# A gelu's square left in its PSUM bank: ScalarE writes it over the product, and VectorE reads it there

## Chip, cores and metric

The kernel runs on one core of one Trainium2 chip. The metric is the device time of one execution in microseconds (us); lower is better. A core has five engines that work side by side: TensorE (PE), which multiplies matrices and writes its products to PSUM; VectorE (DVE); ScalarE (ACT); GpSimd (POOL); and SyncE (SP), whose queue issues here all the transfers (DMAs) between the memory outside the core and SBUF, the core's working memory.

## The reference

```python
def _A_ref(x, wqkv, wo):                      # sliding-window attention: 32 heads of 16, window 256
    qkv = ...(x @ wqkv)...
    scores = einsum("bhqd,bhkd->bhqk", q, k) * Dh ** -0.5
    p = softmax(where(0 <= i - j < 256, scores, -1e9))
    return (p @ v) @ wo

def _B_ref(x, w1, b1, w2, b2):                # dense layer with gelu (tanh form)
    h = gelu(x @ w1 + b1)
    return h @ w2 + b2

g = sigmoid((x * gate_w).sum(-1))
return g * _A_ref(...) + (1 - g) * _B_ref(...)
```

x is 2048 x 512, w1 512 x 1792, w2 1792 x 512, all in float32.

## The kernel before

Dense products are made of three matmuls in a fast 32-bit format (`mm3`, L109 to L111: high times high, high times low, low times high), so each operand is kept as a high and a low part.

The program is one order of instructions written out by hand. Each function, at the point where it is called, emits instructions to the engines' queues; `after(ns, fn)` puts a later step into a list that is ordered by a planned time, and `tick` moves the planned time on. So the place of each instruction on its engine is fixed when the program is built, and on the chip each engine works through its queue in that order, waiting on semaphores.

The work falls into these parts. First come the products with `wqkv` and the transposes of x. From about 150 us on, attention and the dense layer are interleaved. Attention has, for each block of keys, a score matmul whose maximum VectorE takes (tile `sm`, L522; its maximum `jm`, `M`, L527), a second score matmul whose exponential ScalarE takes (tile `st`, L567; exponential `pt`, L589), masks of that exponential on GpSimd (L583), and the products with v (`pv_sm`, `pv_st`, L611). On PE the steps of attention stand between groups of three matmuls of the dense layer. Last comes the product with `wo` and the output.

The dense layer is done in eight turns (`mlp`): a half of the 14 tiles of hidden units, for one of four stretches of 512 rows. A turn has a u stage and a y stage. In the u stage, PE makes seven tiles `u` (128 hidden units x 512 rows, 12 matmuls each), and each goes through `gelu`. In the y stage, PE makes four tiles `y` from the seven results `h`. The tiles u and y take turns in two PSUM banks (pool tag `d`, 2 buffers): the first matmul of a tile has to wait until the tile two places before it has been read for the last time.

`gelu` has seven steps, the first planned at once and the others 700 to 7000 ns after it, by `GELU`:

- L722, ScalarE: x1 = u + b1, from PSUM to SBUF
- L725, ScalarE (f1): the square of (u + b1), from PSUM to the SBUF tile `sq`
- L728, VectorE (f2): sq = (sq + c) * x1
- L731, ScalarE: tanh of it
- L734, VectorE: x1 = (tanh + 1) * x1
- L737, ScalarE, and L740, VectorE: the high and the low part of the result, `h`

The profile calls the tile x1 `x1h` and the tile sq `sqh`. The two buffers of `sq` also hold results of the y stage (`yo`, L815) until they are stored. L183 on VectorE or GpSimd makes the low part of a weight that has landed (`raw_w`), after ScalarE (L179) has made the high part; L665 on VectorE scales an attention result with the reciprocal `rb`, which comes by a DMA.

Of the kernel before, what the change touches and what calls it, by code (L numbers as in the profile page):

```python
# [12 lines left out]
AF = mybir.ActivationFunctionType  # L13
ALU = mybir.AluOpType
# [13 lines left out]
GC = 1.0 / 0.044715  # L28
# [4 lines left out]
def gated_mix(ctx: ExitStack, tc: tile.TileContext, x, wqkv, wo, w1, b1, w2, b2, gate_w, out):  # L33
    nc = tc.nc
# [11 lines left out]
    def f32(ap):  # L46
        return ap.bitcast(F32)
# [26 lines left out]
    b1c = cs.tile([128, NF], F32, name="b1c")  # L74
# [41 lines left out]
    def after(ns, fn, *args):  # L116
        now[1] += 1
        heapq.heappush(todo, (now[0] + ns, now[1], fn, args))
# [599 lines left out]
    def gelu(p, f, h):  # L718

        x1 = sb.tile([128, T], F32, tag="x1", bufs=2, name=f"x1{h.name}")  # L720
        sq = sb.tile([128, T], F32, tag="sq", bufs=2, name=f"sq{h.name}")
        nc.scalar.activation(x1, p, AF.Identity, bias=b1c[:, f:f + 1])  # L722

        def f1():
            nc.scalar.activation(sq, p, AF.Square, bias=b1c[:, f:f + 1])  # L725

        def f2():
            nc.vector.scalar_tensor_tensor(sq, sq, GC, x1, op0=ALU.add, op1=ALU.mult)  # L728

        def f3():  # L730
            nc.scalar.activation(sq, sq, AF.Tanh, scale=GS)  # L731

        def f4():
            nc.vector.scalar_tensor_tensor(x1, sq, 1.0, x1, op0=ALU.add, op1=ALU.mult)  # L734

        def f5():
            nc.scalar.activation(h[:, 0], x1, AF.Copy)  # L737

        def f6():
            nc.vector.tensor_sub(h[:, 1], x1, f32(h[:, 0]))  # L740
            done.add(h.name)
        for ns, fn in zip(GELU, (f1, f2, f3, f4, f5, f6)):
            after(ns, fn)
# [303 lines left out]
```

## Time and profile before

| | |
|---|---|
| median of 3 runs | 749.54 us (749.44 to 749.55) |
| span of the profiled execution, first to last instruction | 747.5 us |
| busy: PE, VectorE, ScalarE, GpSimd | 732.3, 519.5, 421.8, 372.5 us |
| granted clock of TensorE | 1.00 in all stages shown |
| DMA | 172 MB, mean 230 GB/s |

The profiled execution has no run time of its own beside the span of 747.5 us; the 2.0 us up to the median of the runs lie around the first and the last instruction.

How to read it: "busy" is the time in which an engine worked on an instruction. Matmuls are pipelined, so PE can count as busy while the next matmul is held up for a moment. The chain of work that ended last is followed back from the last instruction, at each step to what released it. In a row of a group, `out<-in` are tiles by the program's names, then come their sizes, the count, the busy time in us and the mean time of one in ns, and the idle time of the engine just before them with what ended it. In a row of the timeline, the first number is the start and the second the length, in us; a bracket at the end gives the idle time of the engine before it and what ended that.

### The profile page before, as it was taken

The numbers are of one execution on the slowest core, as the hardware profiler recorded it, in microseconds if no ns is written. First come the engines' busy times: TensorE is split into PE (matmuls) and PEld (weight loads), VectorE is DVE, ScalarE is ACT, GpSimd is POOL, SyncE is SP. The second block draws the span as 40 slices with busy tenths as digits, with TensorE's granted clock in tenths as the row PEclk, the third lists the DMA queues.
The fourth block names the chain that finished last, engine by engine and source line by source line (L and its number), as shares of the span: only waits on it lengthen the run. The fifth ranks groups of instructions, "written<-read, shape, count | busy, mean of one in ns | idle before, by whom it ended". The sixth has DMA issues, their size and how long they took to land.

```text
span 747.5 us, 17960 instructions
## 1 busy us (share of the span) xinstructions
PE 732.3 (98%) x6129; PEld 604.7 (81%) x6129; DVE 519.5 (69%) x1567; ACT 421.8 (56%) x972; POOL 372.5 (50%) x846
## 2 busy tenths in 40 slices
PE   8999999998999999999999999999999999999998
PEld 7888888876788888888887877888888888867786
DVE  4632425799768867886898689768867986784552
ACT  4434532358437835764695478437745853794550
POOL 4200000339756865876587668747765875630000
PEclk9999999999999999999999999999999999999999
DMA  9979898898995687799566889996799789558673
GB/s 318 336 243 408 288 391 282 254 311 194 263 258 132 173 238 205 178 220 265 155 169 156 237 209 232 257 231 154 179 262 238 185 204 287 138 179 230 205 235 113
DMA packets 179259, 172.12 MB, mean 230 GB/s; under 512 B 56672, under 2 KB 122976, under 8 KB 179168
## 3 DMA queue, kind: packets, MB, share of 16 engines
q1 hardware_dynamic: 179168, 170.97, 82.0%
q8 instruction: 49, 0.80, 0.5%
q14 instruction: 42, 0.34, 0.2%
HBM read 108.53 MB, written 62.39 MB: 229 GB/s over the span
## 4 chain that ended last, share of the span: by engine, by line
PE 85%; DVE 4%; DMA 3%; ACT 3%; issue 3%; POOL 1%; SPq 0%; DVEq 0%; ACTq 0%; POOLq 0%
PE sm L522 9%; PE st L567 8%; PE pv_sm L611 7%; PE y L109 7%; PE y L110 6%; PE y L111 6%; PE u L109 5%; PE u L110 5%; PE u L111 5%; PE qk L109 4%; PE qk L111 4%; PE qk L110 4%; PE a L109 2%; PE v L109 2%; PE v L111 2%
## 5 line engine op out<-in xcount | busy, mean ns | idle before, releaser
L527 DVE CUSTOM_DVE_ANT_0 jm<-sm,mask 128x320 bf16<-128x320 f32 (+4 forms) x512 | 237.9, 465 | 95.4 <-PE sm L522 61.0
L583 POOL TENSOR_SCALAR_AFFINE_SELECT pt<-pt 64x256 f32<-64x256 f32 (+1 forms) x538 | 227.6, 443 | 109.4 <-ACT pt L589 99.1
L589 ACT ACTIVATE pt<-st 128x320 f32<-128x320 f32 (+4 forms) x512 | 199.6, 424 | 139.0 <-PE st L567 135.4
L522 PE MATMUL sm<-kd,qd 96*128 96x320 f32 (+4 forms) x512 | 153.9, 312 | 6.9 <-DVE M L527 6.1
L567 PE MATMUL st<-qs,ks 128*128 128x320 f32 (+4 forms) x512 | 154.0, 309 | 1.9 <-ACT pt L589 1.9
L549 POOL CAST qs<-tt 4x256 fp32r<-4x256 f32 x256 | 124.2, 485 | 53.2 <-DVE tt L542 42.6
L522 PEld LDWEIGHTS sm<-kd,qd 96*128 96x128 f32 x512 | 96.4, 188 | 33.6 <-DVE M L527 14.2
L567 PEld LDWEIGHTS st<-qs,ks 128*128 128x128 f32 x512 | 97.1, 190 | 18.9 <-ACT pt L589 3.3
L109 PE MATMUL y<-w,h 128*128 128x512 f32 x224 | 88.6, 395 | 0.0
L110 PE MATMUL y<-w,h 128*128 128x512 f32 x224 | 87.9, 392 | 0.0
L111 PE MATMUL y<-w,h 128*128 128x512 f32 x224 | 87.9, 392 | 0.0
L109 PE MATMUL u<-mx,w 128*128 128x512 f32 x196 | 80.0, 408 | 0.0
L110 PE MATMUL u<-mx,w 128*128 128x512 f32 x196 | 77.3, 395 | 0.0
L111 PE MATMUL u<-mx,w 128*128 128x512 f32 x196 | 77.0, 393 | 0.0
L611 PE MATMUL pv_sm<-pt,vbuf 64*32 64x320 f32 (+4 forms) x1408 | 73.6, 346 | 0.2
L611 PE MATMUL pv_st<-pt,vbuf 64*32 64x320 f32 (+4 forms) x1408 | 73.3, 346 | 0.0
L611 PEld LDWEIGHTS pv_sm<-pt,vbuf 64*32 64x32 f32 x1408 | 50.2, 106 | 20.1 <-issue 2.4
L326 DVE TENSOR_TENSOR qke<-qk,qke 128x512 fp32r<-128x512 f32 x32 | 22.0, 688 | 45.9 <-ACT qke L323 38.5
L323 ACT ACTIVATE qke<-qk 128x512 fp32r<-128x512 f32 x32 | 19.1, 597 | 55.4 <-PE qk L111 32.9
L111 PEld LDWEIGHTS y<-w,h 128*128 128x128 f32 x224 | 42.1, 188 | 9.9
L339 POOL MEMSET vx<- 128x32 f32 x16 | 2.4, 156 | 89.4 <-DMA SQ<-qke 42.4
L611 PEld LDWEIGHTS pv_st<-pt,vbuf 64*32 64x32 f32 x1408 | 46.1, 106 | 0.0
(148 smaller groups left out, 1332.6 us busy)
## 6 DMA issues: line engine op xcount, KB each, us to landing
kd<-SK SPq DMA_DIRECT2D x32, 384.0 KB
qs<-SQ SPq DMA_DIRECT2D x64, 192.0 KB
mx<-XT SPq DMA_DIRECT2D x24, 512.0 KB
SQ<-qke SPq DMA_DIRECT2D x16, 512.0 KB
SK<-qke SPq DMA_DIRECT2D x16, 512.0 KB
ND<-nd SPq DMA_DIRECT2D x32, 256.0 KB
raw_w<-in_B_w_dram SPq DMA_DIRECT2D x28, 256.0 KB
ks<-SK SPq DMA_DIRECT2D x32, 192.0 KB
```

The costliest lines, as they stand in the source:

```text
L109: nc.tensor.matmul(p, lh, rh, start=first, stop=False)
L110: nc.tensor.matmul(p, lh, rl, start=False, stop=False)
L111: nc.tensor.matmul(p, ll, rh, start=False, stop=last)
L323: nc.scalar.activation(e[:, h], p, AF.Copy)
L326: nc.vector.tensor_sub(e[:, 1 - h], p, f32(e[:, h]))
L522: nc.tensor.matmul(p[:, :w], qd[0:96, n, pr, 128 * j:128 * (j + 1)], kd[0:96, n, pr, k1 - w:k1], start=True, stop=True)
L527: nc.vector.tensor_tensor_reduce(junk[:, :w], p[:, :w], mask[:, 320 - w:320], 1.0, -3e38, ALU.add, ALU.max, M[:, 2 * (b % RB) + hb, pr:pr ...
L549: nc.gpsimd.tensor_copy(dst, src.unsqueeze(1).broadcast_to([4, 2, RB, 32]))
L567: nc.tensor.matmul(p[:, :w], ks[:, slot(g_, kb // NB), pr, at:at + 128], qs[:, pr, k0:k0 + w], start=True, stop=True)
L583: nc.gpsimd.affine_select(out=v, in_=v, pattern=[[0, v.shape[1]], [1 - 2 * e, 64]], compare_op=ALU.is_ge, fill=0.0, base=-e, channel_multi ...
L589: nc.scalar.activation(pt[:, hf, pr, :w], p[:, :w], AF.Exp, scale=SCALE)
L611: nc.tensor.matmul(pv[r // 64][32 * i:32 * i + 32, q - c * T:e - c * T], vts[g_, b // NB][r:r + 64, v:v + 32], rhs(r), start=start, stop=s ...
```

## The change

Two lines of `gelu`: ScalarE writes the square over its own input, in the PSUM bank p of the tile u, and VectorE's step f2 reads it there. The tile sq in SBUF is first written by f2.

```diff
         def f1():
-            nc.scalar.activation(sq, p, AF.Square, bias=b1c[:, f:f + 1])
+            nc.scalar.activation(p, p, AF.Square, bias=b1c[:, f:f + 1])

         def f2():
-            nc.vector.scalar_tensor_tensor(sq, sq, GC, x1, op0=ALU.add, op1=ALU.mult)
+            nc.vector.scalar_tensor_tensor(sq, p, GC, x1, op0=ALU.add, op1=ALU.mult)
```

Every engine has the same instructions in the same order as before; operands and waits differ. On PE, in the u stage of the fifth turn (at 441.6 us of the profile before), this is the first matmul of the fourth tile of the turn, u_10, which takes the bank of u_8:

```order
 L522 MATMUL sm_13_2_6384<-kd,qd 128x320 [waits DVE_49]
 L567 MATMUL st_1_3_6389<-qs,ks 128x320 [waits Activation_49]
-L109 MATMUL u_10_6393<-mx_4403,w_10_5446 128x512
+L109 MATMUL u_10_6393<-mx_4403,w_10_5446 128x512 [waits DVE_49]
 L110 MATMUL u_10_6393<-mx_4403,w_10_5446 128x512
 L111 MATMUL u_10_6393<-mx_4403,w_10_5446 128x512
```

It has not moved; it now waits for VectorE, which has to be done with f2 of u_8. Before, it had no mark for ScalarE's f1, which an earlier wait of PE covered. In all, 21 first matmuls of a tile are marked with a wait for VectorE in this way.

On VectorE at the same place, f2 of u_8 stands between the product of an attention result with its reciprocal (L665, which waits for DMAs) and the low part of a weight (L183):

```order
 L527 ISA M_12_6213 128x1
 L665 TENSOR_TENSOR num_1_6194<-num_1_6194,rb_1_6196 128x512 [waits DMAHW7_49,DMAHW0_49]
-L728 SCALAR_TENSOR_TENSOR sqh_8_6322_6329<-sqh_8_6322_6329,x1h_8_6322_6328 128x512 [waits Activation_49]
+L728 SCALAR_TENSOR_TENSOR sqh_8_6322_6329<-u_8_6182,x1h_8_6322_6328 128x512 [waits Activation_49]
 L183 TENSOR_TENSOR w_9_6354<-raw_w_6177,w_9_6354 128x512 [waits DMAHW4_49,Activation_49]
 L527 ISA jm_13_0_6361,M_12_6213<-sm_13_0_6359,mask 128x320 [waits DVE_49,PE_49]
```

Only f2's first input has changed, from the SBUF tile to the bank.

On ScalarE, f1 of the same tile (the second of its turn) had a wait for the store of an earlier result from the buffer of sq; it now has none:

```order
 L722 ACTIVATE x1h_8_6322_6328<-u_8_6182,b1c 128x512
-L725 ACTIVATE sqh_8_6322_6329<-u_8_6182,b1c 128x512 [waits DMAHW3_49]
+L725 ACTIVATE u_8_6182<-u_8_6182,b1c 128x512
 L179 ACTIVATE w_9_6354<-raw_w_6177 128x512 [waits DMAHW4_49]
 L589 ACTIVATE pt_1_6345<-st_1_0_6346 128x320 [waits PE_49,Pool_49]
```

The queues of GpSimd and SyncE are the same to the last wait.

## The prediction

> **What bounds the kernel now.** I read the page first: busy time, then the chain of work that ended last, then the groups. After that came the stages, and last the moments at which TensorE (PE) stood still. A quoted row begins with its start in us from the span's start, then its length in us.
>
> ```profile
> span 747.5 us, 17960 instructions
> ...
> PE   732.3 (98%) x6129; PEld 604.7 (81%) x6129; DVE 519.5 (69%) x1567; ACT 421.8 (56%) x972; POOL 372.5 (50%) x846
> ...
> PE 85%; DVE 4%; DMA 3%; ACT 3%; issue 3%; POOL 1%; SPq 0%; DVEq 0%; ACTq 0%; POOLq 0%
> ```
>
> PE carries 85% of the chain, and an instruction that is not on PE counts only where PE waits for it. VectorE (DVE) is busy 69% on average. The stages differ (columns: stretch, its length, then busy us of PE, weight loads, DVE, ScalarE (ACT), GpSimd (POOL)):
>
> ```profile
> 254.00:288.00 34.00, 34.00 (x343) 28.43 (x341) 23.54 (x83) 16.05 (x39) 22.93 (x60) 1.00 0.87 243
> ...
> 426.00:459.00 33.00, 31.49 (x303) 25.30 (x303) 28.46 (x89) 24.81 (x57) 20.70 (x43) 1.00 0.85 214
> ```
>
> The first is a stage of second matmuls (y) with hardly any gelu: PE never stops. The second is a stage of first matmuls (u) with gelu: DVE is 86% busy and PE idle 1.5 us. What the change can move lies in the u stages.
>
> **The change, part by part.** I call the square f1 (L725, ACT) and the step that reads it f2 (L728, DVE). No instruction is added, removed or moved: PE, DVE, ACT, POOL and SP (with every DMA) issue the same list. Three things differ.
>
> *f2 reads one operand from PSUM.* Its group (busy us and mean ns), and min/median/max ns of it and of a relative:
>
> ```profile
> L728 DVE SCALAR_TENSOR_TENSOR sqh<-sqh,x1h 128x512 f32<-128x512 f32 x56 | 42.5, 759 | 2.8 <-ACT sqh L725 2.2
> ```
>
> ```profile
> L728 DVE SCALAR_TENSOR_TENSOR sqh<-sqh,x1h x56: 651/692/1578, 156.0 to 671.8; 128x512 f32<-128x512 f32 x56
> ```
>
> ```profile
> L815 DVE SCALAR_TENSOR_TENSOR yo<-y,ya x32: 651/685/692, 197.5 to 697.7; 128x512 f32<-128x512 f32 x32
> ```
>
> L815 is f2's operation with its first input in PSUM and its second in SBUF, which is what f2 becomes. Its minimum and median are f2's, but it is never above 692 ns, while f2, with both inputs in SBUF, reaches 1578. I take 685: 56 x (759 - 685) = 4.1 us of DVE time, of which only what PE waits for counts. Bounds for one f2: 651 from below, and from above 752, from the output's step, which reads PSUM too but takes a column as its scalar:
>
> ```profile
> L882 DVE SCALAR_TENSOR_TENSOR ao<-a,g,ao x17: 483/750/752, 703.3 to 744.4; 128x512 f32<-128x512 f32 x15, 128x256 f32<-128x256 f32 x2
> ```
>
> Which slowed f2 stands in an unbroken run of DVE work that PE then waits for? Five. The largest:
>
> ```profile
> 159.75 1.58 DVE L728 SCALAR_TENSOR_TENSOR sqh<-sqh,x1h 128x512 f32<-128x512 f32 x1
> ```
>
> ```profile
> 159.28 1.51 POOL L183 TENSOR_TENSOR w<-raw_w,w 128x512 fp32r<-128x512 f32 x1 [6.88 <-ACT w L179]
> ```
>
> ```profile
> 161.80 0.42 PE L522 MATMUL sm<-kd,qd 96*128 96x320 f32 x1 [0.67 <-DVE M L527]
> ```
>
> ```profile
> 172.40 0.63 ACT L179 ACTIVATE w<-raw_w 128x512 fp32r<-128x512 f32 x1 [0.49 <-DMA raw_w<-in_B_w_dram]
> ```
>
> f2 runs beside a POOL instruction of 1.5 us, and PE's score matmul (sm) waits behind it: 1.58 - 0.685 = 0.9 us. But at 172.40 ACT waits for a weight to land, which may take the lead back; I count half, 0.45, and keep 0 and 0.9 as ends. The others:
>
> ```profile
> 441.41 0.88 DVE L728 SCALAR_TENSOR_TENSOR sqh<-sqh,x1h 128x512 f32<-128x512 f32 x1
> ...
> 442.06 0.40 PE L111 MATMUL u<-mx,w 128*128 128x512 f32 x1
> ...
> 443.22 0.07 DVE L527 DVE_READ_ACCUMULATOR2_ANT M<- 128x1 f32 x1
> ...
> 443.35 0.41 PE L522 MATMUL sm<-kd,qd 96*128 96x320 f32 x1 [0.89 <-DVE M L527]
> ```
>
> ```profile
> 466.46 0.85 DVE L728 SCALAR_TENSOR_TENSOR sqh<-sqh,x1h 128x512 f32<-128x512 f32 x1
> ```
>
> ```profile
> 467.78 0.41 PE L522 MATMUL sm<-kd,qd 96*128 96x320 f32 x1 [0.62 <-DVE M L527]
> ```
>
> ```profile
> 394.97 0.77 DVE L728 SCALAR_TENSOR_TENSOR sqh<-sqh,x1h 128x512 f32<-128x512 f32 x1
> ```
>
> ```profile
> 398.93 0.41 PE L522 MATMUL sm<-kd,qd 96*128 96x320 f32 x1 [0.91 <-DVE M L527]
> ```
>
> ```profile
> 594.83 0.88 DVE sqh L728
> ...
> 604.32 0.72 POOL pt L583
> ```
>
> Against 0.685 they give 0.20, 0.17, 0.08 and 0.20. The last stands in the chain, which goes from it over ACT to POOL's masks, for which the next p.v matmuls wait. Sum of f2: 0.45 + 0.65 = 1.10 us. Where these waits go, PE's own stream is late next.
>
> *f1 writes PSUM.* No ACT instruction here writes PSUM. The nearest rows are a read that changes side:
>
> ```profile
> L323 ACT ACTIVATE qke<-qk 128x512 fp32r<-128x512 f32 x32 | 19.1, 597 | 55.4 <-PE qk L111 32.9 <-issue 10.8 <-DMA SQ<-qke 2.6
> ...
> L731 ACT ACTIVATE sqh<-sqh 128x512 f32<-128x512 f32 x56 | 35.3, 631 | 1.8 <-DVE sqh L728 1.7
> L725 ACT ACTIVATE sqh<-u,b1c 128x512 f32<-128x512 f32 x56 | 38.8, 693 | 0.0
> ...
> L233 ACT ACTIVATE ks<-nil,own 128x512 fp32r<-128x512 f32 x8 | 5.3, 724 | 0.0
> ```
>
> Reading PSUM in place of SBUF is 34 ns shorter; I take as much for the write. Ends: 597 (the fastest full-width activation, -96) and 724 (the slowest, +31). On the chain f1 stands 8 times in a piece of over 0.3 us; first and last:
>
> ```profile
> 186.53 0.59 ACT sqh L725
> ...
> 670.12 0.58 ACT sqh L725
> ```
>
> 8 x 34 = 0.27 us gained, with ends of +0.25 (longer) and -0.77. The waits that f1 loses, for the store of an earlier result from its old buffer, f2 had already; no idle time of ACT stood before f1 (0.0 above), so they cost nothing and give nothing.
>
> *The bank comes free later.* Two PSUM banks serve u and y in turn, so the first matmul of the tile after next waited for f1, and now for f2. Queued behind it on PE are the sm and st matmuls of attention, and behind those the maxima on DVE and the exponentials on ACT. I set the end of all 56 f2 against the first matmul that takes over their bank. In 53 f2 ends sooner, the tightest of these by 0.28 us:
>
> ```profile
> 662.02 0.88 DVE L728 SCALAR_TENSOR_TENSOR sqh<-sqh,x1h 128x512 f32<-128x512 f32 x1
> ```
>
> ```profile
> 663.18 0.40 PE L109 MATMUL u<-mx,w 128*128 128x512 f32 x1
> ```
>
> The three late ones, beside the f2 of 441.41 above:
>
> ```profile
> 441.60 0.39 PE L109 MATMUL u<-mx,w 128*128 128x512 f32 x1
> ```
>
> ```profile
> 666.72 0.42 DVE L577 TENSOR_TENSOR pt<-pt,cut 128x256 f32<-128x256 f32 x1
> 667.05 0.68 DVE L728 SCALAR_TENSOR_TENSOR sqh<-sqh,x1h 128x512 f32<-128x512 f32 x1
> ```
>
> ```profile
> 667.01 0.39 PE L109 MATMUL y<-w,h 128*128 128x512 f32 x1
> ...
> 671.08 0.41 PE L567 MATMUL st<-qs,ks 128*128 128x320 f32 x1 [1.20 <-ACT pt L589]
> ```
>
> ```profile
> 166.26 0.68 DVE L728 SCALAR_TENSOR_TENSOR sqh<-sqh,x1h 128x512 f32<-128x512 f32 x1
> ...
> 166.76 0.39 PE L109 MATMUL u<-xt,w 128*128 128x512 f32 x1
> ```
>
> ```profile
> 170.88 0.39 PE L567 MATMUL st<-qs,ks 128*128 128x320 f32 x1 [0.40 <-ACT pt L589]
> ```
>
> f2 ends at 442.29, 667.73 and 166.94: PE is late by 0.69, 0.72 and 0.18 us, plus 0.06 each to hear of it (443.29 to 443.35, above): 1.77 in all. Each cover is a wait of PE soon after it. At 443.35 the sm waits for DVE work queued behind this same f2; at 671.08 an st waits 1.20 for ACT; at 170.88 one waits 0.40. All are longer than the lateness, so I take 0; with the covers gone it is 1.77. The reason is general: an f2 is late when DVE is behind, and then its maxima are late too, for which PE waits anyway.
>
> A rule that speaks against the change is in the Trainium skill, "Perfetto Trace Analysis", section "Optimizing Scalar/DVE Operations": an access costs VectorE about 60 ns in SBUF and about 125 in PSUM, and ScalarE about 93 and 51. By it f2 would be 65 ns longer than an unslowed one and f1 42 shorter. An estimate from these figures, at the places above (f2 at 0.75 there), is 0.79 + 8 x 0.042 = 1.13 us less, 748.4. The L815 row disagrees for VectorE (685 against 692 in the median); the 34 ns are near its ScalarE difference.
>
> **The sum.** 1.10 + 0.27 - 0 = 1.37 us less. The profiled execution spans 747.5 us; the runs' median is 749.54, and I take the 2.0 us around the span as unchanged. 749.54 - 1.37 = 748.2.
>
> **The rivals.**
>
> (a) *More than the counted places gain.* DVE leads the u stages at 86%, and a DVE lead carries from one wait to the next. If half of the 4.1 us and the whole 0.27 reach the end, it is 749.54 - 2.3 = 747.2. Against it: even in the u stage shown, DVE is idle 14% of the time, and a lead ends at the next idle time. 17 in 100.
>
> (b) *Hidden anyway.* The lead at 161.80 is lost at 172.40, later ones to DMA landings like the one DVE waits for ahead of the f2 of 441.41: 749.54 - 0.3 = 749.2.
>
> ```profile
> 440.76 0.72 DVE L665 TENSOR_TENSOR num<-num,rb 128x512 f32<-128x512 f32 x1 [1.35 <-DMA rb<-RD]
> ```
>
> 11 in 100.
>
> (c) *PE waits for f2: slower.* The same row shows the danger: f2 can stand behind a DMA, and PE then waits for the bank. If none of the three is covered, and only 0.3 of the gains remains, 749.54 + 1.77 - 0.3 = 751.0. It decides from the point where the next wait of PE is shorter than f2's lateness. 17 in 100.
>
> (d) *PSUM reads are slow on DVE.* With f2 at 0.75, the five places give 0.41 (half of 0.83), 0.13, 0.10, 0.02 and 0.13, with f1's 0.27 together 1.06 us: 748.5. The L815 row speaks against it; 3 in 100.
>
> My forecast has 52 in 100, half of it on each side of 748.04, since the start's 0.9 comes whole or not at all. About 0.2% (1.5 us) is what a measurement of this kernel tells from no change. Faster: 26 + 17 = 43; within: 26 + 11 + 3 = 40; slower: 17. Range: 746.6, below (a), to 751.0, at (c).
>
> **What would show it.** f2's maximum at or below 700 ns and its mean near 685; f1 at 655 to 665; the idle time before the sm at 161.80 gone; rows of PE u or y L109 that wait for DVE sqh L728, under 1 us in all, and behind each a wait of PE that is shorter than before. The prediction is wrong if those waits sum to over 2 us, if f1 is over 724 ns, or if DVE falls by 4 us and PE's idle time does not move.

## The result, and the profile after

The change makes the kernel faster: 744.98 us in the median of six runs (743.49 to 745.76), against 749.54 for the kernel before (748.57 to 751.22). The ratio is 0.993, with a 95% interval of 0.9915 to 0.9945. The forecast was 748.2, and the range ended at 746.6: the sign was right, but the gain is 4.6 us and not 1.4. The profiled run of the changed kernel took 745.76, the slowest of its six, so the two traces show only 3.5 us of the 4.6 (spans of 747.5 and 744.0). In the runs of the changed kernel the time is 1.7 to 1.8 us longer than the span, so the profiled execution of the kernel before, with no run time of its own, stands for one of about 749.3 us.

The page of the changed kernel, with span, busy time and the shares of the chain:

```profile
span 744.0 us, 17964 instructions
...
PE 731.7 (98%) x6129; PEld 604.6 (81%) x6129; DVE 513.6 (69%) x1567; ACT 421.0 (57%) x972; POOL 356.9 (48%) x846
...
PE 86%; DVE 4%; DMA 4%; ACT 3%; issue 2%; SPq 1%; DVEq 0%; ACTq 0%
```

PE works as long as before. DVE is 5.9 us less busy, and POOL, none of whose instructions was touched, is 15.6 us less busy (372.5 before). That second number is the surprise. The same two stretches as before, a y stage and a u stage:

```profile
254.00:288.00 34.00, 34.00 (x342) 28.45 (x341) 23.86 (x86) 15.02 (x38) 22.97 (x61) 1.00 0.88 239
...
426.00:459.00 33.00, 32.00 (x303) 25.23 (x302) 28.86 (x90) 25.63 (x57) 22.65 (x46) 1.00 0.85 206
```

PE's idle time in the u stage went from 1.5 to 1.0 us (the same stretch of time; the changed kernel is some 3 us further in its work there). The two edited instructions, f2 and then f1 (least, median and greatest ns):

```profile
L728 DVE SCALAR_TENSOR_TENSOR sqh<-u,x1h x56: 652/685/694, 156.1 to 667.2; 128x512 f32<-128x512 f32 x56
```

```profile
L725 ACT ACTIVATE u<-u,b1c x56: 642/662/744, 154.6 to 665.5; 128x512 f32<-128x512 f32 x56
```

No f2 is held up any more: the greatest fell from 1578 to 694. What PE waited for (us in total, times, longest), first before, then after:

```profile
PE sm L522 <- DVE M L527: 6.1, 11, 1.0
PE st L567 <- ACT pt L589: 1.9, 3, 1.2
```

```profile
PE sm L522 <- DVE M L527: 3.0, 7, 0.8
...
PE st L567 <- ACT pt L589: 1.0, 3, 0.5
PE y L109 <- DVE sqh L728: 0.6, 1, 0.6
...
PE u L109 <- DVE sqh L728: 0.4, 1, 0.4
```

The waits for maxima and exponentials fell by 4.0 us, and the new waits for the bank are 1.0. GpSimd's masks as a group, before and after (busy us and mean ns of one):

```profile
L583 POOL TENSOR_SCALAR_AFFINE_SELECT pt<-pt 64x256 f32<-64x256 f32 (+1 forms) x538 | 227.6, 443 | 109.4 <-ACT pt L589 99.1
```

```profile
L583 POOL TENSOR_SCALAR_AFFINE_SELECT pt<-pt 64x256 f32<-64x256 f32 (+1 forms) x538 | 215.3, 420 | 119.0 <-ACT pt L589 108.6
```

The same 538 masks take 12.3 us less. I sorted them, by the start and end of each, into those that overlap an f2 by more than 50 ns and the rest. Before, 47 lay beside one, with a mean of 613 ns, and the rest had 426. After, 57 lie beside one, with a mean of 389, and the rest have 424.

The rest is not undisturbed: many of these masks run beside another DVE step that reads two tensors from SBUF (L734, L740, L183, L665, L577). Take the 334 masks of 64x256 alone. Before, 215 of them overlap neither an f2 nor one of these steps, and each takes 406 to 419 ns; the other 119 take 640 in the mean. After, with f2 no longer one of the steps with two tensors in SBUF, 252 are clear of such steps, again 406 to 419 ns each, and 82 are not, with 638. The 30 that meet the new f2 and no such step take 410.5 in the mean, as if f2 were not there. So a mask beside a step with two tensors in SBUF is as slow as before; there are fewer of them.

**Where the time came from.** I set the start of every first matmul (L109) after against the same one before. PE's lead in us, at times of the kernel before:

| at | lead | what added to it |
|---|---|---|
| 162 | 0.9 | f2 of 159.75 no longer held up |
| 176 | 1.8 | the subtraction L740 of 172.88 no longer held up |
| 189 | 2.1 | small steps |
| 234 | 2.4 | p.v matmuls that waited for masks |
| 395 | 3.4 | 0.4 at 322 and 0.4 at 394.5, where an sm had waited for a maximum, and small steps |
| 441.6, then 444.4 | 3.0, then 3.7 | from 3.5: a wait for the bank, given back at once, and 0.2 more as the f2 of 441.41 is not held up |
| 468 | 3.7 | 0.2 gained at 458, 0.4 lost at 465 to 467, 0.15 gained behind the f2 of 466.46 |
| 607 | 4.4 | p.v matmuls that waited for masks |
| 667.0, then 671.3 | 3.8, then 4.5 | a wait for the bank, given back at once |
| 716 to the end | 3.6 | a matmul of the last product waits for DVE |

The second step was not in the forecast. Before, a subtraction on DVE stood beside one on POOL, and an sm waited behind it:

```profile
172.49 1.29 POOL L183 TENSOR_TENSOR w<-raw_w,w 128x512 fp32r<-128x512 f32 x1
...
172.88 1.45 DVE L740 TENSOR_TENSOR h<-x1h,h 128x512 fp32r<-128x512 f32 x1
...
175.61 0.41 PE L522 MATMUL sm<-kd,qd 96*128 96x320 f32 x1 [0.63 <-DVE M L527]
...
189.44 0.40 PE L109 MATMUL y<-w,h 128*128 128x512 f32 x1
```

After, DVE's step has come 1.0 us earlier and POOL's subtraction 1.85 us earlier, and they meet for only 0.07 us (the last row is the y matmul of 189.44):

```profile
170.64 1.30 POOL L183 TENSOR_TENSOR w<-raw_w,w 128x512 fp32r<-128x512 f32 x1
...
171.87 0.69 DVE L740 TENSOR_TENSOR h<-x1h,h 128x512 fp32r<-128x512 f32 x1
...
187.37 0.39 PE L109 MATMUL y<-w,h 128*128 128x512 f32 x1
```

Nor was the step at 394.5. There, two DVE steps that the change does not edit, an L183 and an L734, stood beside masks, and an sm waited behind them; before, then after:

```profile
393.11 0.89 DVE L734 SCALAR_TENSOR_TENSOR x1h<-sqh,x1h 128x512 f32<-128x512 f32 x1
...
394.46 0.42 PE L522 MATMUL sm<-kd,qd 96*128 96x320 f32 x1 [0.28 <-DVE M L527]
```

```profile
389.92 0.68 DVE L734 SCALAR_TENSOR_TENSOR x1h<-sqh,x1h 128x512 f32<-128x512 f32 x1
...
391.00 5.33 POOL L583 TENSOR_SCALAR_AFFINE_SELECT pt<-pt 64x256 f32<-64x256 f32 x12 [1.89 <-ACT pt L589]
...
391.07 0.41 PE L522 MATMUL sm<-kd,qd 96*128 96x320 f32 x1
```

POOL had done its masks early and stood idle for 1.89 us, so L734 ran alone (0.68 us in place of 0.89), and the L183 before it too (0.69 in place of 0.85).

The block of masks for which the p.v matmuls of 607 wait, before and then after:

```profile
599.41 5.86 POOL L583 TENSOR_SCALAR_AFFINE_SELECT pt<-pt 64x256 f32<-64x256 f32 x12 [0.90 <-ACT pt L589]
```

```profile
595.42 4.98 POOL L583 TENSOR_SCALAR_AFFINE_SELECT pt<-pt 64x256 f32<-64x256 f32 x12 [1.43 <-ACT pt L589]
```

Twelve masks in 4.98 us in place of 5.86. Last, the bank at its worst place, after:

```profile
663.24 0.50 PE L109 MATMUL y<-w,h 128*128 128x512 f32 x1 [0.62 <-DVE sqh L728]
...
666.53 0.42 PE L567 MATMUL st<-qs,ks 128*128 128x320 f32 x1 [0.50 <-ACT pt L589]
...
712.75 0.50 PE L109 MATMUL a<-wo,ot 128*128 128x512 f32 x1 [0.83 <-DVE ao L882]
```

PE waits 0.62 for f2; the st behind it then waits 0.50 where it waited 1.20 before. The last row is the wait at the end that takes 1.0 us of the lead back.

### The profile page after: what moved, and what is told of

It reads as the page before. It is cut to its first block, busy times and chain, and to the rows that moved or that the text cites. A ratio compares the mean times of both kernels' runs of the same rounds, so it can differ in the third digit from the quotient of the medians.

```text
span 744.0 us, 17964 instructions
## 1 busy us (share of the span) xinstructions
PE 731.7 (98%) x6129; PEld 604.6 (81%) x6129; DVE 513.6 (69%) x1567; ACT 421.0 (57%) x972; POOL 356.9 (48%) x846
## 4 chain that ended last, share of the span: by engine, by line
PE 86%; DVE 4%; DMA 4%; ACT 3%; issue 2%; SPq 1%; DVEq 0%; ACTq 0%
PE sm L522 9%; PE st L567 8%; PE pv_sm L611 7%; PE y L109 7%; PE y L110 7%; PE y L111 7%; PE u L109 6%; PE u L110 5%; PE u L111 5%; PE qk L109 4%; PE qk L111 4%; PE qk L110 4%; PE v L109 2%; PE v L111 2%; PE v L110 2%; PE pv_st L611 2%
## 5 line engine op out<-in xcount | busy, mean ns | idle before, releaser
L583 POOL TENSOR_SCALAR_AFFINE_SELECT pt<-pt 64x256 f32<-64x256 f32 (+1 forms) x538 | 215.3, 420 | 119.0 <-ACT pt L589 108.6
L549 POOL CAST qs<-tt 4x256 fp32r<-4x256 f32 x256 | 120.3, 470 | 55.1 <-DVE tt L542 44.6
L109 PE MATMUL y<-w,h 128*128 128x512 f32 x224 | 88.6, 396 | 0.6 <-DVE sqh L728 0.6
L109 PE MATMUL u<-mx,w 128*128 128x512 f32 x196 | 80.1, 409 | 0.4 <-DVE sqh L728 0.4
L111 PEld LDWEIGHTS y<-w,h 128*128 128x128 f32 x224 | 42.1, 188 | 9.8
L109 PEld LDWEIGHTS y<-w,h 128*128 128x128 f32 x224 | 42.4, 189 | 4.6 <-DVE sqh L728 0.8
```

The costliest lines, as they stand in the source:

```text
L109: nc.tensor.matmul(p, lh, rh, start=first, stop=False)
L111: nc.tensor.matmul(p, ll, rh, start=False, stop=last)
L549: nc.gpsimd.tensor_copy(dst, src.unsqueeze(1).broadcast_to([4, 2, RB, 32]))
L583: nc.gpsimd.affine_select(out=v, in_=v, pattern=[[0, v.shape[1]], [1 - 2 * e, 64]], compare_op=ALU.is_ge, fill=0.0, base=-e, channel_multi ...
```

## The experiments

The theory, from the two traces: f2 with both inputs in SBUF and GpSimd's instructions beside it hold each other up; with one input in PSUM neither is held up, and the gain comes on both sides. The rivals: ScalarE's write to PSUM is what helps; VectorE's shorter mean time is what helps; the gain belongs to the start alone; something in the later release of the bank reorders waits in a lucky way. Ratios are to the kernel before on the same chip, with 95% intervals.

**f2 reads PSUM, f1 does not write it.**

```diff
-            nc.scalar.activation(p, p, AF.Square, bias=b1c[:, f:f + 1])
+            nc.scalar.activation(sq, p, AF.Square, bias=b1c[:, f:f + 1])
-            nc.vector.scalar_tensor_tensor(sq, p, GC, x1, op0=ALU.add, op1=ALU.mult)
+            nc.vector.scalar_tensor_tensor(sq, sq, GC, p, op0=ALU.add, op1=ALU.mult)
```

> One part of the change alone: f1 writes its square to the SBUF tile as before, and f2 takes the product in PSUM as its second factor in place of x1 (b1 is left out of this one factor), so f2 has one input in PSUM and one in SBUF and f1 is as slow as before (689 ns). Port theory (the time comes from f2 and GpSimd's masks no longer slowing each other, because f2 no longer reads two inputs from SBUF): f2 never above 700 ns, masks beside f2 near 390 ns in place of 613, and nearly the whole gain: 3.0 to 4.5 us less than before, a ratio of 0.994 to 0.996. Write theory (the time comes from f1's shorter write, 56 x 27 ns): no gain, 0.999 to 1.001.

Measured: 745.71, ratio 0.9939 (0.992 to 0.9959). f2, and the masks:

```profile
L728 DVE SCALAR_TENSOR_TENSOR sqh<-sqh,u x56: 648/682/691, 156.0 to 666.2; 128x512 f32<-128x512 f32 x56
```

```profile
L583 POOL TENSOR_SCALAR_AFFINE_SELECT pt<-pt 64x256 f32<-64x256 f32 (+1 forms) x538 | 215.5, 421 | 117.0 <-ACT pt L589 106.6
```

f1 writes SBUF again (691 ns in the median), and nearly the whole gain stays, with the masks as short as in the changed kernel. ScalarE's write is not the cause.

**The first turn alone, and the other seven alone.** In `gelu`, f1's output and f2's first input are p only for n == 0, or only for n > 0:

```diff
-            nc.scalar.activation(p, p, AF.Square, bias=b1c[:, f:f + 1])
+            d = p if n == 0 else sq
+            nc.scalar.activation(d, p, AF.Square, bias=b1c[:, f:f + 1])
```

> The change in the seven tiles of the first turn alone (150 to 185 us). If the lead that PE gets there is kept (the traces differ by 2.07 us at the first y matmul, 189 us): 1.5 to 2.2 us less, 0.997 to 0.998. If the weight that lands at 172.40 takes it back, as one half of the prediction's sum had it: 0 to 0.5 us less, 0.9995 to 1.000.

> The change in the 49 tiles of the other seven turns alone. If gains add up along PE: the rest of the 4.5 us that the traces differ by at 671 us, 2.0 to 2.5 us less, 0.9965 to 0.9975. By the prediction's count of places (0.65 + 0.24 us): 0.9 us less, 0.999.

Measured: the first turn alone 747.98, ratio 0.999 (0.9971 to 1.0008), which shows no gain for certain; the other seven 747.09, ratio 0.9958 (0.9943 to 0.9972), or 2.1 to 4.3 us. The median of the first turn alone is 1.5 us below that of the kernel before, at the edge of the first expectation, but the interval holds no gain as well. The seven turns bring much more than the 0.9 that the forecast counted for them. The first turn's lead does arise (PE gains 2.1 us between 150 us and the matmul of 189.44), but in the profiled run of that kernel 1.1 us of it is lost soon after, at a matmul that waits:

```profile
203.45 0.41 PE L522 MATMUL sm<-kd,qd 96*128 96x320 f32 x1 [0.97 <-PE y L111]
```

The y that the row names had ended 0.97 us before; what this sm waited for, a transfer perhaps, the profile does not show.

**VectorE's mean time restored, the square still in PSUM.** A column in place of the constant makes f2 longer (the gelu's own constant is thereby left out, here and in the next two kernels):

```diff
-            nc.vector.scalar_tensor_tensor(sq, p, GC, x1, op0=ALU.add, op1=ALU.mult)
+            nc.vector.scalar_tensor_tensor(sq, p, b1c[:, f:f + 1], x1, op0=ALU.add, op1=ALU.mult)
```

> The changed kernel with a column of b1 in place of f2's constant (a wrong constant, so the gelu is not the reference's), which should make every f2 about 750 ns long, as the output's step with a column is: VectorE's mean time for f2 is then that of before (759), but f2 still has only one tensor input in SBUF. If only VectorE's own time counts: the gain is nearly gone, 0 to 1 us less than before, 0.999 to 1.000. If what counts is that no single f2 is held up for long and GpSimd's masks are not held up: 2 to 4 us less, 0.995 to 0.997, with masks beside f2 near 390 ns.

Measured: 746.24, ratio 0.9947 (0.9927 to 0.9968).

```profile
L728 DVE SCALAR_TENSOR_TENSOR sqh<-u,b1c,x1h x56: 707/746/752, 156.4 to 668.1; 128x512 f32<-128x512 f32 x56
```

```profile
596.10 5.00 POOL L583 TENSOR_SCALAR_AFFINE_SELECT pt<-pt 64x256 f32<-64x256 f32 x12 [1.37 <-ACT pt L589]
```

f2's mean is 745 ns, against 759 before, so nearly the whole shortening of the mean is gone; most of the gain stays. What counts is not f2's mean but that f2 no longer has its hold-ups and no longer holds POOL up: the masks at 596 take 5.00 us, as in the changed kernel. The intervals of this kernel and the changed one overlap, so what the 60 ns per f2 cost is not measured.

**The bank held, the square in SBUF; and the same without holding the bank.** Both are the kernel before with another scalar in f2. In the first it is a column of the bank, which keeps the bank until f2 has ended; in the second a column in SBUF:

```diff
-            nc.vector.scalar_tensor_tensor(sq, sq, GC, x1, op0=ALU.add, op1=ALU.mult)
+            nc.vector.scalar_tensor_tensor(sq, sq, p[:, 0:1], x1, op0=ALU.add, op1=ALU.mult)   # first
+            nc.vector.scalar_tensor_tensor(sq, sq, b1c[:, f:f + 1], x1, op0=ALU.add, op1=ALU.mult)   # second
```

> The price of the later release alone. f1 writes SBUF and f2 reads both tensors from SBUF as before; in place of its constant f2 takes column 0 of the product's bank (a wrong constant, so the gelu is not the reference's), which keeps the bank until f2 is done. The same as e6 but for the place of the column. If the release costs nothing (the prediction's third term): within 0.5 us of e6. If PE's waits come through to the end: 1.8 us or more above e6.

> The control of e5 and e4: the kernel before with a column of b1 from SBUF in place of f2's constant (a wrong constant). f2 still has two tensor inputs in SBUF and should take 750 ns alone and more beside GpSimd. If VectorE's own time counts: slower than before by up to 56 x 65 ns = 3.6 us, of which a third to a half reaches the end, 750.5 to 751.5. By the port theory, which leaves the contention in place: 0 to 2 us slower, and 3 to 5 us above e4, from which it differs only in where the square lies.

Measured: 750.8 with the bank held, ratio 1.0009 (0.9991 to 1.0027), and 750.42 without, 1.0012 (0.9998 to 1.0026). f2 and the masks of the second:

```profile
L728 DVE SCALAR_TENSOR_TENSOR sqh<-sqh,b1c,x1h x56: 709/752/1735, 156.3 to 674.6; 128x512 f32<-128x512 f32 x56
```

```profile
L583 POOL TENSOR_SCALAR_AFFINE_SELECT pt<-pt 64x256 f32<-64x256 f32 (+1 forms) x538 | 228.1, 444 | 110.4 <-ACT pt L589 99.4 <-issue 0.4
```

Holding the bank is worth 0.4 us by the medians, with intervals that overlap: nothing that can be told from zero. And this second kernel differs from the one with the column before it (746.24) only in where the square lies. That alone is 4.2 us by the medians, taken on two chips (by the ratios to the kernel before on each chip, 0.0065 or 4.9 us), with the hold-ups (1735) and the long masks (444) on the side of SBUF.

**GpSimd's subtractions given to VectorE**, in the kernel before and in the changed one:

```diff
-            after(LAND + 1500, split, key, nc.gpsimd if key[1] % 2 else nc.vector)
+            after(LAND + 1500, split, key, nc.vector)
```

> The kernel before, with the low parts of the first weights of the dense layer (L183, 120 to 190 us) all on VectorE; before, every second one was on GpSimd, where one takes 1.3 us and reads two inputs from SBUF. Five of them move, at some 0.7 us each on VectorE. If it is GpSimd's subtraction that holds up the f2 of 159.75 (1578 ns) and the last step of 172.88 (1449 ns): no f2 and no L740 above 950 ns, and the first y matmul near 188 us in place of 189.4; in the time 0.5 to 1.5 us less if that lead is kept, 0 if it is not. If those two were slow for another reason: both stay above 1400 ns, and the time is 0 to 2 us longer.

> The same edit on the changed kernel, whose f2 has one input in SBUF and is not held up beside GpSimd's subtraction. If the two edits remove the same hold-up: within 1 us of the changed kernel, 744 to 746, so the gain of the edit on the kernel before does not come on top. If they add up: 743.5 or less.

Measured on the kernel before: 749.63, ratio 1.0004 (0.9991 to 1.0017).

```profile
L728 DVE SCALAR_TENSOR_TENSOR sqh<-sqh,x1h x56: 648/692/922, 157.2 to 672.4; 128x512 f32<-128x512 f32 x56
```

With POOL's subtractions gone, f2's 1578 is gone too: they were its cause. What is left, up to 922, lies beside the masks L583 and GpSimd's small copies (L549). The time did not follow: VectorE took on five subtractions, and PE, which waits for maxima between 130 and 150 us, is already 1.2 us late at 150, before the first f2. From there to the y matmul of 189.44 it gains 0.7, so that this matmul comes at 189.94 and not, as was expected, near 188. On the changed kernel the edit gives 747.28, ratio 0.9969 (0.9949 to 0.9989): 2.3 us of the median are lost, which neither expectation had, and the start's lead at 189 is gone (that matmul comes at 189.46). So POOL's subtractions are best left on POOL, with f2 out of their way. That edit could not say what the start is worth by itself, since it moves work to VectorE.

**The next step of the gelu too.** The tanh is written into the bank and L734 reads it there, with the later steps of `GELU` planned closer (2400, 3200, 5000, 6000 in place of 3600, 4600, 6000, 7000); the control has the closer steps alone:

```diff
-            nc.scalar.activation(sq, sq, AF.Tanh, scale=GS)
+            nc.scalar.activation(p, sq, AF.Tanh, scale=GS)
-            nc.vector.scalar_tensor_tensor(x1, sq, 1.0, x1, op0=ALU.add, op1=ALU.mult)
+            nc.vector.scalar_tensor_tensor(x1, p, 1.0, x1, op0=ALU.add, op1=ALU.mult)
```

> The changed kernel in which the tanh too is written over the bank and the next VectorE step (f4) reads it there, with the gelu's steps planned closer together (tanh at 2400 in place of 3600 ns, f4 at 3200 in place of 4600, the last two at 5000 and 6000). f4 leaves the contention too (748 to 685 ns in the mean, and its masks), but the bank is held some 3 us longer. By the port theory alone: 1 to 3 us less than e8. If the bank now decides: PE waits for f4 in many of the 56 tiles, 3 us or more above e8.

> The control of e7: the changed kernel with the gelu's steps planned closer together and nothing else. The steps that VectorE and ScalarE have to do stay the same, so both theories expect it within 1.5 us of the changed kernel, 743.5 to 746.5.

Measured: 760.67, ratio 1.0159 (1.0129 to 1.0189); the control 744.84, 0.9927 (0.9904 to 0.9951).

```profile
PE u L109 <- DVE x1h L734: 14.7, 21, 1.9
...
PE y L109 <- DVE x1h L734: 3.8, 4, 1.2
```

Here the bank decides: PE waits 18.5 us for L734, and the kernel is 15.8 us slower than its control, although POOL is freed further (336.2 us busy). Rival (c) of the forecast was a true mechanism; f2 merely ends early enough to stay clear of it, and L734 does not.

**The same with a third bank**, taken from st, and the control with the third bank alone:

```diff
-            p = ps.tile([128, T], F32, tag="d", bufs=2, name=f"u{t}_{f}")
+            p = ps.tile([128, T], F32, tag="d", bufs=3, name=f"u{t}_{f}")
-        p = ps.tile([128, 320], F32, tag="st", bufs=3, name=f"st{g_}_{kb}_{i}")
+        p = ps.tile([128, 320], F32, tag="st", bufs=2, name=f"st{g_}_{kb}_{i}")
```

> As e7 (tanh and f4 in the bank as well), but with the gelu's steps planned as in the changed kernel and a third bank for u and y, taken from the score tiles st, which keep two of three. If e7's price is the bank alone: the waits of PE for f4 (18.5 us in e7) fall below 3 us, and the time is within 2 us of e12 or below it. If f4's chain itself is the price: waits of PE for VectorE of over 8 us remain.

> The control of e11: the changed kernel with three banks for u and y and two for st. f2's release has slack everywhere, so by the prediction's third term (waits for f2 cost nothing) nothing is gained there; attention loses a buffer. If st's third buffer matters: 1 to 6 us above the changed kernel, 746 to 751.

Measured: 748.71, ratio 0.9984 (0.9969 to 0.9999); the control 749.53, 0.9997 (0.9984 to 1.001). The control's wait for exponentials:

```profile
PE st L567 <- ACT pt L589: 8.0, 14, 1.2
```

PE no longer waits for L734, but st, with two buffers, now makes it wait 8.0 us in the control, and 6.9 in the kernel with L734 in PSUM, where the changed kernel has 1.0. Taking the bank from st costs 4.5 us by the medians; with L734 in PSUM the pair is 0.8 apart, with intervals that overlap. No version tried is clearly ahead of the changed kernel.

## Why the prediction was right or wrong

*Right: f2's own time.* It was to have a maximum at or below 700 ns and a mean near 685; the maximum is 694 and the mean 684. The Trainium skill, "Perfetto Trace Analysis", section "Optimizing Scalar/DVE Operations", has an access to PSUM dearer for VectorE by some 65 ns; the median of 685 against 692 disagrees, and the row of L815 was the better guide.

*Right: the bank.* The term was 0. PE falls back at all three places named, by 0.54, 0.77 and 0.23 us, where the forecast had 0.75, 0.78 and 0.24. Behind each a wait of PE became shorter, as forecast (0.89 to 0.04 us at 443.35, 1.20 to 0.50 at 671.08, 0.40 to 0.18 at 170.88), and made it good, the third to within 0.1 us. Holding the bank with the square in SBUF costs 0.4 us by the medians.

*Right in size, and minor: f1.* Its mean fell from 693 to 665 ns, 28 against the 34 taken; the kernel without f1's write to PSUM has nearly the whole gain.

*Wrong: the term of f2, 1.10 us.* PE's lead at 662 us is 4.5. The step that failed is the question by which the places were chosen, which slowed f2 stands in an unbroken run of DVE work that PE then waits for, with its answer of five. It put at nothing what the change does to instructions that are not edited, and waits that PE's rows do not show. At the five places the count itself held: followed from matmul to matmul, PE gains 0.94 us behind the f2 of 159.75, 0.21 behind that of 441.41, 0.15 (466.46), 0.07 (394.97) and 0.33 (594.83). That is 1.7 us, where the forecast had 1.55 with the start taken whole and 1.10 in its sum. The other 2.8 us of the lead, net, came from elsewhere, in three ways.

First, the count took f2's own shortening and not what f2 did to its neighbours. The forecast saw that f2 ran long beside an instruction of POOL, and took POOL as the cause and DVE as the one that suffers. Both suffer. The masks beside an f2 took 613 ns, and p.v matmuls wait for masks: these gain 0.27 us at 232 and 0.33 at 605, where the forecast had nothing and 0.20. In the trace of before this could have been read by asking POOL the question that was asked of DVE: how long is a mask beside a step with two tensors in SBUF (640 ns for 64x256), and how long clear of one (411). The Trainium skill, "SBUF — State Buffer", section "Who interferes with whom", says that a VectorE instruction with two inputs in SBUF contends with a GpSimd instruction that reads SBUF, and one with at most one such input does not. The trace agrees: 613 ns became 389, and 1578 became 694.

Second, the start was halved for the transfer of 172.40, but its lead doubled instead. Both engines came early to the next meeting, L740 of 172.88 beside POOL's next subtraction, and POOL by more than DVE, so they hardly met: 1449 ns became 689, and PE gained another 0.87 us. A step that is moved in time meets other neighbours, and that can give as well as take.

Third, PE's lead grew in the other turns where the count had no place. At 394.46 it grew by 0.44 us, from L183 and L734, which stood clear of masks in their new time. At 322 it grew by 0.36: the f2 of 320.14 and the L665 behind it, which reads two tensors from SBUF as well, each took 0.2 us less. PE's rows show no idle time above 0.01 us at that place, since the matmuls overlap, but the weight loads of the two sm there had waited 0.31 and 0.28 us for a maximum. In all, the waits of these weight loads for maxima fell from 14.2 to 8.8 us, more than the 6.1 to 3.0 of PE's rows. Two more steps are 0.21 at 458 and 0.13 at 528; at 465 to 467, 0.39 was lost. The seven turns together gave 2.1 to 4.3 us.

Rival (a) had the right sign and reason, a lead that carries on from wait to wait, but priced it from DVE's 4.1 us alone, so that the range ended too high.

*Open.* How the gain splits between POOL's shorter masks and DVE's missing hold-ups: each was shown to go and come with the place of the square, but no run took away one without the other. In the two traces, PE gains 0.6 us where it had waited for masks, and most of the rest where it had waited for DVE; but at 394.5, for one, DVE was faster because POOL had done its masks early. Whether the start's lead always lasts: the first turn alone showed no certain gain. The 1.0 us that the last product takes back belongs to the profiled run of the changed kernel, the slowest of its six; in the profiled runs of the kernels with f2's second factor in PSUM, with the column, with the closer steps and with the subtractions moved, that wait is 0.2 us, as in the kernel before. Why it was longer there is not known.

## What to carry to other kernels

When a VectorE instruction with two SBUF inputs is at times far longer than its median, look at what GpSimd runs beside it, and compare GpSimd's own instructions beside and clear of it: the price is paid on both sides, and the busy time of an engine that the edit does not touch belongs in the sum. Moving one of the two inputs to PSUM takes the hold-up away at no cost in length, as long as the bank is free before the next matmul wants it; one step further along the same chain cost 15.8 us. Places counted singly, at the edited instruction and at idle time of PE, give a floor: each was about right here, but together they were 1.7 of 4.5 us. The rest came from instructions that were not edited, which met other neighbours in their new time, and from waits that show in the weight loads alone, so the range has to leave room for them on the side of the gain.

## What was not expected of the hardware

- GpSimd's masks are held up by f2 as f2 is by them: 613 ns beside an f2 with two SBUF inputs, and 389 beside one that reads PSUM. What decides is whether a DVE step beside the mask reads two tensors from SBUF, whichever step it is: a mask of 64x256 takes 640 ns in the mean beside one, and 406 to 419 clear of all of them.
- Beside one of GpSimd's subtractions of 1.3 to 1.5 us, a DVE step of 685 ns took 1449 and 1578. Beside masks and the copies L549 (0.3 to 0.9 us each) it took up to 942: f2 and L740 had 33 steps of 800 ns or more before, the two long ones included, and 6 after, all of them L740, whose inputs still lie both in SBUF. L734, which reads two tensors from SBUF in both kernels, had 15 before and 16 after.
- A column as f2's scalar costs 60 ns more than a constant, whether the input lies in PSUM (746 against 685) or in SBUF (752 against 692).
